# A channel mixer and a state-space convolution in one instruction order: GpSimd makes the weights' low parts from slot 14 on, two table loads are booked, and the order is drawn up again

## The chip, the cores and the metric

The kernel runs on one core of one Trainium2 chip. The metric is the device time of one launch in microseconds (us). Before the change three runs gave 1084.74, 1084.84 and 1085.39 us, with a median of 1084.84 us.

Five engines work at once, each through its own queue in program order: PE (TensorE: matmuls, with its weight loads shown as PEld), DVE (VectorE), ACT (ScalarE), POOL (GpSimd) and SP (which only issues DMAs here). POOL and ACT issue DMAs too. An instruction waits on semaphores for what other engines must have done, and everything behind it in its own queue waits with it.

## The reference

The reference normalises the 2048 rows of `u` (576 channels each) and sends them down two branches. One is a state-space convolution over the sequence (an S4D layer, by FFT), the other a two-layer mixer with 4608 hidden units:

```python
def reference(A_u, A_log_A_real, A_A_imag, A_C_real, A_C_imag, A_log_dt, A_D_skip, B_x, B_w1, B_b1, B_w2, B_b2):
    def _A_ref(u, log_A_real, A_imag, C_real, C_imag, log_dt, D_skip):
        L = u.shape[1]
        dt = jnp.exp(log_dt)
        A = -jnp.exp(log_A_real) + 1j * A_imag
        C = (C_real + 1j * C_imag) * dt[:, None]
        pos = (lambda x, dt: x.astype(dt))(jnp.arange(L), log_dt.dtype)
        P = jnp.exp((A * dt[:, None])[:, :, None] * pos[None, None, :])
        K = 2.0 * jnp.einsum("dn,dnl->dl", C, P).real
        ...
        y = jnp.fft.irfft(Uf * Kf[None, :, :], L2)[:, :, :L]
        ...
        return y + u * D_skip[None, None, :]

    def _B_ref(x, w1, b1, w2, b2):
        y = _layernorm(x, axis=-1)
        h = _gelu(jnp.einsum("bsd,df->bsf", y, w1) + b1)
        return jnp.einsum("bsf,fd->bsd", h, w2) + b2

    x = A_u
    xn = _layernorm(x, axis=-1)
    s = _A_ref(xn, A_log_A_real, A_A_imag, A_C_real, A_C_imag, A_log_dt, A_D_skip)
    g = _silu(_B_ref(xn, B_w1, B_b1, B_w2, B_b2))
    return x + s * g
```

All of it is in float32. `L` is 2048, `D` 576, `N` 128.

## The kernel before

**The mixer.** Float32 accuracy is reached with products of two parts each: a value is rounded to a high part (type fp32r) and the rest becomes a low part, and three products (high by high, high by low, low by high) are added. The mixer goes through its rows in two halves, and in each half through the 4608 hidden units in 12 groups `g` of 384, each group for two row blocks `tb` of 512. That makes 48 *slots* (`NSLOT`). A slot has 11 *positions*: three units of layer 1 (`layer1`, L508, 14 matmuls of 512 columns each, 42 in a slot) and eight of layer 2 (`layer2`, L565, 72 matmuls of 288 columns in a slot). Between them ACT applies the gelu (L541) and makes the high part `hh` (L544), and DVE makes the low part `hl` (L547). DVE adds each finished layer-2 sum to `acc` (L573). The sums lie in two PSUM tiles, `mxa` and `mxb`, which change turns, so an add has to be done before PE writes that tile again.

**The weights.** They change every second slot. A DMA on SP's queue brings a piece into `raw` (`load_raw`, L448 to L453); ACT rounds it to the high part (`split_raw`, L488) and an engine given as `low_on` subtracts to get the low part (L485). Each pair of slots has eight such pieces: five of w1 (`w1l`, 128x384; the fifth, `w1s`, has 64 partitions) and three of w2 (`w2l`, 128x576). The tiles are single, so w1's pieces are made while layer 2 of the odd slot runs, and w2's while layer 1 of the next slot runs. `split_raw(low_on=nc.vector)` defaults to DVE; only three pieces at the start are given to GpSimd. Once a low part is done, `low()` issues the next loads into the ring that it has read (`NEXT`), and these wait on SP's queue for it.

**The convolution.** It is filled in between. Its tables come from 36 blocks (`tables`: some eleven DVE and four ACT instructions each, L785 to L827), from which PE makes a piece of the kernel (`kgen`, L867, 64 small matmuls, called K below). Six chunks of 96 channels then pass forward transforms (`forward`, L939), products (`s2`, L977, with DVE L993 to L1006), inverse steps (L1030) and a last one (`i1`, L1057), whose result goes to DRAM by POOL's queue (L1068).

**The order.** One fixed order of instructions for all engines is written out by a planner, `Order`, while the kernel is traced. It holds a clock per engine (`od.t`), *lines* of steps with an engine, an estimated duration, a due time (`by`) and marks that steps need, and `od.tbl`, the activation table that ACT has by its book: a step with another `tbl` is booked with 1.28 us more. `weigh_in` books the eight weight pieces with due times counted back from the position that needs them. `od.advance` gives engines such steps as are ready and don't run into the next due time. The real hardware then runs this order with semaphores; where its times differ from the planner's, an engine waits.

**PE's visits to the convolution.** `pe_turns` runs after certain positions (`all_lines=pos in (0, 1, G + 1, G + 4, NPOS - 1)`, with `G` = 3 and `NPOS` = 11). It takes a step of the convolution when it is ready by the planner's clock. Forward and product steps (line `c1`) are held to a pace (`END`, and a share of the mean gap). A K can *ride* ahead of such a step in the same visit (`ride`, `lead`); it goes alone only when it has been ready for `ALONE` us:

```python
                if x is kl and pace["started"] and kl["steps"][0]["mark"][1] < NB - 1 and od.t["PE"] < h[1] + ALONE:
                    break
```

**Tables on ACT.** In the parameters' steps an arctangent (L709) is followed by an absolute value (L710) and a sine (L711); both functions are booked as one table, "sin". In slots 22 and 23 the finished mixer rows pass the gate's tanh (`tanh_half`, L578, booked as table "gelu"), and DVE's L589 follows.

Of the kernel before, what the change touches and what calls it, by code (L numbers as in the profile page):

```python
# [12 lines left out]
AF = mybir.ActivationFunctionType  # L13
# [22 lines left out]
G = 3  # L36
# [6 lines left out]
def dve(n):  # L43
    return 0.075 + 0.00104 * n


def act(n):
    return 0.06 + 0.00098 * n
# [159 lines left out]
def step(eng, dur, fn, need=(), mark=None, cv=0, at=0.0, late=0.0, tbl=None, by=1e9):  # L208
    return dict(eng=eng, dur=dur, fn=fn, need=tuple(need), mark=mark, cv=cv, at=at, late=late, tbl=tbl, by=by)
# [3 lines left out]
def mixer_kernel(ctx, tc, u, log_a_real, a_imag, c_real, c_imag, log_dt, d_skip, w1, b1, w2, b2,  # L213
# [249 lines left out]
    def split_raw(low_on=nc.vector):  # L463
        k = state["split"]
        state["split"] += 1
        half, g, which, i = PARTS[k]
        r = RAW.pop(k)
        if which == 1:
            if i == 0 and k:
                w1_tiles()  # L470
            h, lo, r1, r2 = W[1]
            if i < KB:
                h, lo = h[:, i], lo[:, i]
                m = P
            else:
                h, lo = r1, r2[:64]
                m = 64
        else:
            if i == 0:
                W[2] = (sb.tile([P, G, D], F32R, name="w2h"), sb.tile([P, G, D], F32R, name="w2l"))  # L480
            h, lo = W[2]
            h, lo, m = h[:, i], lo[:, i], P

        def low():
            low_on.tensor_sub(lo, r[:m], h[:m].bitcast(F32))  # L485
            for _ in range(NEXT[which - 1][i]):
                load_raw()
        nc.scalar.activation(h, r, AF.Copy)  # L488
        return low
# [85 lines left out]

    def tanh_half(z):
        t = sb.tile([P, TB], F32, name="h32", bufs=2)[:, :288]
        nc.scalar.activation(t, z, AF.Tanh, scale=0.5)  # L578
        return t

# [83 lines left out]
    def params():  # L664
# [41 lines left out]
            add("DVE", 1.9, lambda h=h: V.reciprocal(t[:, h], t[:, h]))  # L706
        add("DVE", d, lambda: V.scalar_tensor_tensor(ci, T[4], 1.0, ci, op0=OP.subtract, op1=OP.mult))
        add("DVE", d, lambda: V.tensor_mul(t, t, ci))
        add("ACT", e, lambda: A.activation(t, t, AF.Arctan), tbl="sin", late=0.0)  # L709
        add("ACT", e, lambda: A.activation(T[3], t, AF.Abs))  # L710
        add("ACT", e, lambda: A.activation(T[3], T[3], AF.Sin, bias=halfpi[:, 0:1], scale=-2.0), tbl="sin", late=0.0)  # L711
        turns(1, th)
# [456 lines left out]
    L1 = 14 * 0.2262  # L1169
    LEN = [L1] * G + [3 * n * 0.1327 for n in (4, 2, 2, 4, 3, 3, 3, 3)]  # L1170

    T0 = 12.5
    for e, t in dict(PE=0.0, ACT=4.6, DVE=3.7, POOL=3.8, SP=0.0).items():
        od.t[e] = T0 + t
    for x in od.lines:
# [86 lines left out]
        od.force(lambda: ("y2", tb, KB) in od.marks)  # L1262
        od.marks["x", tb] = od.marks["y2", tb, KB]

    def weigh_in(which):

        m = KB + 1 if which == 1 else G
        end = od.t["PE"] + sum(LEN[G:] if which == 1 else LEN[:G])
        for i in range(m):
            by = end - 0.8 * (m - i)  # L1270
            cell = []
            n = G * P if which == 1 else D
            k = len(WM)
            WM.append(which)
            wl["steps"].append(step("ACT", act(n), lambda c=cell: c.append(split_raw()), need=[("raw", k)],
                                    mark=("wh", k), by=by - 0.9, at=od.t["PE"] + od.LAT))

            def low(c=cell, k=k, n=n):
                k0 = state["load"]
                c[0]()  # L1280
                for j in range(k0, state["load"]):
                    od.marks["raw", j] = od.t["DVE"] + dve(n) + 5.5 + 1.0 * (j - k0)
            wl2["steps"].append(step("DVE", dve(n), low, need=[("wh", k)], mark=("w", k), by=by))

    WM = [1] * (KB + 1)
    for k in range(len(WM)):
# [64 lines left out]


    pace = dict(left=NCH * (2 + 2 + 4), last=0.0, started=False)
    END = 1020.0
    ALONE = 3.0

    def pe_turns(limit=1, any_time=False, all_lines=True):
        for x in (nl, pl, ml) + ((c3, c1, kl) if all_lines else ()):
            n = 0
            while n < (2 if x in (c1, nl) else limit):  # L1360
                h = od.head(x)
                if h is None or h[0]["eng"] != "PE" or h[1] > od.t["PE"] + (0.3 if x is nl else -0.2):
                    break
                if x is c1:
                    now = od.t["PE"]
                    gap = (END - now) / max(pace["left"], 1)
                    if n == 0 and pace["started"] and now < pace["last"] + 0.4 * gap and not any_time:
                        break
                    pace["started"], pace["last"] = True, now
                    pace["left"] -= 1  # L1370
                if x is kl and pace["started"] and kl["steps"][0]["mark"][1] < NB - 1 and od.t["PE"] < h[1] + ALONE:
                    break
                behind = ride(h[0]) if x is c1 or x is c3 and h[0]["mark"][0] == "i1" else None
                od.run(x)
                if behind:
                    behind()
                od.pin()
                od.advance(od.t["PE"])
                n += 1
# [52 lines left out]
    for slot in range(NSLOT):  # L1432
        turn[0] = slot + 1
        g, tb = slot // 2 % NG, slot % 2
        n = slot // 2
        final = slot >= NSLOT - 2
        for pos in range(NPOS):
            if pos < G:
                need = wmark(n, 1) + [("x", tb)]
                if pos == 0:  # L1440
                    if slot in (mid, mid + 1):
                        x_ready(tb)
                    od.force(lambda: all(m in od.marks for m in need))

                    if slot in (1, 2 * NG + 1):
                        od.marks["x", tb] -= 2.3
                cell = []
                od.unit(lambda: cell.extend([layer1(g, tb, pos)] if slot else first_layer1(pos)),
                        L1 if slot else L1 * (22, 6, 14)[pos] / 14, need)
                look_ahead(pos)  # L1450
                for k, (a, b, c) in enumerate(cell, pos + 1 - len(cell)):
                    by = hidden_by(pos, k)
                    od.urgent.append((od.t["PE"], [step("ACT", 0.62, a, tbl="gelu", by=by[0]),
                                                   step("ACT", act(TB), b, by=by[1]),
                                                   step("DVE", dve(TB), c, mark=("h", slot, k), by=by[2])]))
                od.advance(od.t["PE"])
                if pos == G - 1 and tb == 1 and slot + 1 < NSLOT:
                    weigh_in(1)
            else:
                j, terms, last, hid = l2_terms(pos - G)  # L1460
                need = [wmark(n, 2)[i] for i in hid] + [("h", slot, i) for i in hid]
                if pos == G:

                    pe_turns()
                od.force(lambda: all(m in od.marks for m in need))
                if max(od.marks[m] for m in need) > od.t["PE"] + 0.3:
                    pe_turns(any_time=True)
                cell = []
                halves = slot == NSLOT - 1 and j == 3
                od.unit(lambda: cell.append(layer2(g, tb, j, terms, last, halves)), LEN[pos], need)  # L1470
                look_ahead(pos)
                if last or halves:
                    add = cell[0]
                    dh, k = (terms[0][1], 1) if halves else (0, 2)
                    done = ("acc", slot, j, dh)
                    chain = [step("DVE", dve(288 * k), lambda: add(dh, k), mark=done, by=add_by(pos, j))]
                    if final:
                        b = 8 + 4 * tb + j
                        x = el if slot < NSLOT - 1 else od.line()
                        st = finish(b, dh * 288, (dh + k) * 288, slot == NSLOT - 1, slot == NSLOT - 1 and j > 1)  # L1480
                        st[0]["need"] = (done, ("s8", b - 8))
                        x["steps"] += st
                    elif g == NG - 1:
                        for d in range(2):
                            one, two = gate_store(4 * tb + j, d)
                            by = od.t["PE"] + 5.0
                            chain += [step("ACT", act(288), one, tbl="gelu", by=by), step("DVE", dve(288), two, by=by)]
                    od.urgent.append((od.t["PE"], chain))
                if pos == NPOS - 1 and tb == 1 and slot + 1 < NSLOT:
                    weigh_in(2)  # L1490
            for f in LATER.get((slot, pos), ()):
                f()
            od.advance(od.t["PE"])
            pe_turns(all_lines=pos in (0, 1, G + 1, G + 4, NPOS - 1))
    od.force(lambda: not od.urgent and not any(x["steps"] for x in od.lines))


# [52 lines left out]
```

## Time and profile before

| what | us |
|---|---|
| median of three runs | 1084.84 |
| the profiled execution, whole | 1084.85 |
| its span, first to last instruction | 1083.1 |
| outside of the span | 1.75 |
| PE busy | 1072.6 |
| DVE busy | 947.7 |
| ACT busy | 653.0 |
| POOL busy | 199.4 |

The profiled execution's time is the median to within 0.01 us, so sums made against it hold for the runs. Its clock was granted in full (0.998). A matmul's shown duration overlaps with the next one's, since they are pipelined. How fast PE works is therefore read from the distance of two starts, and "busy" doesn't tell a late matmul from one in time. In a view by lines, a row gives the line, engine, operation, what is written and read, shape and count, then busy time and the mean of one, then the idle time before and what ended it.

### The profile page before, as it was taken

What the parts mean: (1) busy time and instruction counts of PE and PEld (TensorE: products, weight loads), DVE (VectorE), ACT (ScalarE), POOL (GpSimd) and SP (SyncE); (2) the same over time, 40 slices, a digit from 0 to 9 for tenths busy, and PEclk for the clock granted to TensorE, in tenths of its full rate; (3) what the DMA queues carried; (4) which work ended last, traced back from release to release, by engine and by line L of the source; (5) the groups of instructions that cost most, each with busy time, mean ns of one, the idle gap of its engine ahead of it and who ended that gap; (6) DMA issues with size and microseconds to landing.
All of it is one profiled execution on the core that took longest, in us unless ns stands there. A gap on an engine that the chain in (4) does not pass through costs nothing.

```text
span 1083.1 us, 27198 instructions
## 1 busy us (share of the span) xinstructions
PE 1072.6 (99%) x11491; PEld 933.4 (86%) x11491; DVE 947.7 (88%) x1518; ACT 653.0 (60%) x974; POOL 199.4 (18%) x281
## 2 busy tenths in 40 slices
PE   9999999999999999999999999999999999999997
PEld 7989999889888888888888888888888887888896
DVE  7797878989999999999999999999999996677367
ACT  6558569767666665767756667566665754233333
POOL 6559342110000200002000010000100022110231
PEclk9999999999999999999999999999999999999999
DMA  7746455823225222454423432142312347332344
GB/s 235 231 138 191 152 196 192 215 85 116 71 70 108 67 80 58 108 94 128 134 68 99 83 85 83 37 124 47 107 53 76 111 88 238 111 105 88 96 153 117
DMA packets 136537, 125.54 MB, mean 116 GB/s; under 512 B 88156, under 2 KB 108096, under 8 KB 135392
## 3 DMA queue, kind: packets, MB, share of 16 engines
q1 hardware_dynamic: 120624, 76.44, 26.4%
q0 software_dynamic: 15040, 46.40, 13.7%
q8 instruction: 90, 1.47, 0.6%
q10 hardware_dynamic: 752, 0.97, 0.3%
q14 instruction: 31, 0.25, 0.1%
HBM read 95.52 MB, written 34.01 MB: 120 GB/s over the span
## 4 chain that ended last, share of the span: by engine, by line
PE 87%; DVE 3%; ACT 1%; issue 1%; DMA 1%; POOL 0%; ACTq 0%; DVEq 0%; POOLq 0%
PE mxa L565 19%; PE mxb L565 19%; PE mxa L508 19%; PE mxb L508 19%; PE cv L977 3%; PE cv L867 3%; PE cv L1030 2%; PE cv L939 2%; PE cv L1057 1%; DMA xn_s<-w 0%; DVE hl L547 0%; ACT L541 0%; DVE acc L573 0%; DVE A L644 0%; ACT A L741 0%
## 5 line engine op out<-in xcount | busy, mean ns | idle before, releaser
L565 PE MATMUL mxa<-w2h,hh 128*128 128x288 f32 x573 | 171.4, 299 | 0.0
L565 PE MATMUL mxb<-w2h,hh 128*128 128x288 f32 x576 | 170.9, 297 | 0.0
L565 PE MATMUL mxb<-w2h,hl 128*128 128x288 f32 x576 | 170.1, 295 | 0.2 <-DVE hl L547 0.2
L565 PE MATMUL mxb<-w2l,hh 128*128 128x288 f32 x576 | 169.5, 294 | 0.0
L565 PE MATMUL mxa<-w2h,hl 128*128 128x288 f32 x573 | 169.1, 295 | 0.0
L565 PE MATMUL mxa<-w2l,hh 128*128 128x288 f32 x573 | 168.7, 294 | 0.0
L547 DVE TENSOR_TENSOR hl<-h,hh 128x512 fp32r<-128x512 f32 x144 | 99.4, 692 | 76.3 <-ACT hh L544 75.7
L541 ACT ACTIVATE h<-mxa,b1t 128x512 f32<-128x512 f32 x73 | 50.2, 689 | 126.5 <-PE mxa L508 121.8
L767 POOL DMA_DIRECT2D par<-par_s x36 | 27.3, 759 | 518.9 <-DVE mg L810 479.1
L565 PEld LDWEIGHTS mxa<-w2h,hh 128*128 128x128 f32 x573 | 107.6, 188 | 9.6 <-issue 6.0
L565 PEld LDWEIGHTS mxb<-w2h,hh 128*128 128x128 f32 x576 | 108.2, 188 | 4.9 <-issue 2.5
L565 PEld LDWEIGHTS mxb<-w2l,hh 128*128 128x128 f32 x576 | 108.1, 188 | 0.6
L565 PEld LDWEIGHTS mxb<-w2h,hl 128*128 128x128 f32 x576 | 108.1, 188 | 0.4 <-DVE hl L547 0.4
L565 PEld LDWEIGHTS mxa<-w2l,hh 128*128 128x128 f32 x573 | 107.6, 188 | 0.7
L565 PEld LDWEIGHTS mxa<-w2h,hl 128*128 128x128 f32 x573 | 107.5, 188 | 0.0
L541 ACT ACTIVATE h<-mxb,b1t 128x512 f32<-128x512 f32 x71 | 48.9, 689 | 75.9 <-PE mxb L508 73.7
L544 ACT ACTIVATE hh<-h 128x512 fp32r<-128x512 f32 x144 | 90.9, 632 | 4.0
L573 DVE TENSOR_TENSOR acc<-mxa,acc 128x576 f32<-128x576 f32 x88 | 65.4, 743 | 17.0 <-PE mxa L565 16.7
L508 PE MATMUL mxa<-XH,w1h 128*128 128x512 f32 x284 | 80.3, 404 | 0.0
L508 PE MATMUL mxb<-XH,w1h 128*128 128x512 f32 x280 | 77.3, 398 | 0.2 <-ACT h L541 0.2
L508 PE MATMUL mxa<-XL,w1h 128*128 128x512 f32 x284 | 76.2, 390 | 0.0
L508 PE MATMUL mxa<-XH,w1l 128*128 128x512 f32 x284 | 76.0, 389 | 0.0
(230 smaller groups left out, 2422.3 us busy)
## 6 DMA issues: line engine op xcount, KB each, us to landing
raw<-in_B_w_dram SPq DMA_DIRECT2D x72, 288.0 KB, 3.5
raw<-in_B_w_dram SPq DMA_DIRECT2D x96, 192.0 KB, 3.0
par_s<-A POOLq DMA_DIRECT2D x8, 1080.0 KB, 5.9
par<-par_s POOLq DMA_DIRECT2D x36, 240.0 KB, 3.4
f2t<-f2q SPq DMA_DIRECT2D x24, 256.0 KB, 3.7
raw<-in_B_w_dram SPq DMA_DIRECT2D x48, 96.0 KB, 3.5
u_s<-in_A_u_dram POOLq DMA_DIRECT2D x16, 288.0 KB, 4.4
xc<-xn_s SPq DMA_DIRECT2D x48, 96.0 KB, 3.9
```

The costliest lines, as they stand in the source:

```text
L508: nc.tensor.matmul(q, a, b, start=j == 0, stop=j == len(ops) - 1)
L541: nc.scalar.activation(t, q, AF.Gelu_apprx_tanh, bias=b1t[:, g * G + i:g * G + i + 1], scale=1.0)
L544: LAST[0] = nc.scalar.activation(hh[:, i], t, AF.Copy)
L547: nc.vector.tensor_sub(hl[:, i], t, hh[:, i].bitcast(F32))
L565: nc.tensor.matmul(q[:, dh, :288], a[:, i, c], b[:, i, d], start=i == 0 and k == 0, stop=i == G - 1 and k == 2)
L573: nc.vector.tensor_add(o, q[:, dh:dh + n, :288], b if g == 0 else o)
L767: nc.gpsimd.dma_start(PAR[b].rearrange("p (g i) k -> p g (i k)", g=4), dram(par_s, (b // 6 * CH + b % 6 * 4) * NPAR, [[D * NPAR, P], [24 * ...
L867: nc.tensor.matmul(q[32 * g:32 * g + 32, i // 2, i % 2 * 64:i % 2 * 64 + 64], U[:, ri, 4 * g + i, :], v[:, ri, 4 * g + i, :], start=ri == ...
L939: nc.tensor.matmul(Q1ST[i, x][g // 2][64 * f:64 * f + 64, g % 2].rearrange(order), f1t[r].rearrange("p s k -> p (s k)"), rhs(r, f), start= ...
L977: nc.tensor.matmul(Q[i][32 * q:32 * q + 32, f, 2 * ri:2 * ri + 2], m[r, 4 * i + q, 32 * ri:32 * ri + 32], A2[r, 4 * p + 2 * i + q // 2, :, ...
L1030: nc.tensor.matmul(QI[q // 2][64 * f:64 * f + 64, q % 2, i], MAT["g2t", p + i // 2][r, i % 2, ri], YS[p + i // 2][0][r, i % 2, ri, f], sta ...
L1057: nc.tensor.matmul(Q[f][32 * e:32 * e + 32, t], g1t[r], A2[r, k:k + 2, 1].rearrange("p i d r -> p i r d"), start=True, stop=True, skip_gro ...
```

## The change

It has three parts. From slot 14 on, `weigh_in` gives the low parts of the weights to GpSimd, booked with 0.2 + 0.0023 n us. The arctangent is booked under a table of its own, and where the table booked isn't "gelu", the gate's tanh is preceded by a gelu of one column, which makes the gelu table the one loaded. The planner's constants are new: its start `T0`, the pace (`END`, the share 0.30), `ALONE`, how long before PE's clock a step must be ready (0.60 instead of 0.2), and the positions after which all lines are asked.

```diff
     def tanh_half(z):
         t = sb.tile([P, TB], F32, name="h32", bufs=2)[:, :288]
+        if od.tbl != "gelu":
+            nc.scalar.activation(small[:, 5:6], epst[:, 0:1], AF.Gelu_apprx_tanh)
         nc.scalar.activation(t, z, AF.Tanh, scale=0.5)
         return t
...
-        add("ACT", e, lambda: A.activation(t, t, AF.Arctan), tbl="sin", late=0.0)
+        add("ACT", e, lambda: A.activation(t, t, AF.Arctan), tbl="arctan", late=0.0)
...
-    T0 = 12.5
+    T0 = 13.2
...
-    def weigh_in(which):
-
+    SHIFT = 14
+
+    def weigh_in(which, slot=0):
+
+        e = "POOL" if slot >= SHIFT else "DVE"
         m = KB + 1 if which == 1 else G
         end = od.t["PE"] + sum(LEN[G:] if which == 1 else LEN[:G])
         for i in range(m):
-            by = end - 0.8 * (m - i)
             cell = []
             n = G * P if which == 1 else D
+            d = dve(n) if e == "DVE" else 0.2 + 0.0023 * n
+            by = end - max(0.8, d) * (m - i)
             k = len(WM)
             WM.append(which)
-            wl["steps"].append(step("ACT", act(n), lambda c=cell: c.append(split_raw()), need=[("raw", k)],
+            wl["steps"].append(step("ACT", act(n), lambda c=cell: c.append(split_raw(nc.gpsimd if e == "POOL" else nc.vector)), need=[("raw", k)],
                                     mark=("wh", k), by=by - 0.9, at=od.t["PE"] + od.LAT))
 
-            def low(c=cell, k=k, n=n):
+            def low(c=cell, k=k, d=d):
                 k0 = state["load"]
                 c[0]()
                 for j in range(k0, state["load"]):
-                    od.marks["raw", j] = od.t["DVE"] + dve(n) + 5.5 + 1.0 * (j - k0)
-            wl2["steps"].append(step("DVE", dve(n), low, need=[("wh", k)], mark=("w", k), by=by))
+                    od.marks["raw", j] = od.t[e] + d + 5.5 + 1.0 * (j - k0)
+            wl2["steps"].append(step(e, d, low, need=[("wh", k)], mark=("w", k), by=by))
...
-    END = 1020.0
-    ALONE = 3.0
+    END = 1010.0
+    ALONE = 7.0
...
-                if h is None or h[0]["eng"] != "PE" or h[1] > od.t["PE"] + (0.3 if x is nl else -0.2):
+                if h is None or h[0]["eng"] != "PE" or h[1] > od.t["PE"] + (0.3 if x is nl else -0.60):
                     break
...
-                    if n == 0 and pace["started"] and now < pace["last"] + 0.4 * gap and not any_time:
+                    if n == 0 and pace["started"] and now < pace["last"] + 0.30 * gap and not any_time:
...
-                    weigh_in(1)
+                    weigh_in(1, slot)
...
-                    weigh_in(2)
+                    weigh_in(2, slot)
...
-            pe_turns(all_lines=pos in (0, 1, G + 1, G + 4, NPOS - 1))
+            pe_turns(all_lines=pos in (0, 1, 2, G + 1, G + 3, NPOS - 1))
```

## The prediction

> **What bounds the kernel now.** I read the page first, then PE by lines and by its chain, then the places where PE changes between mixer and convolution, and last what DVE and POOL do beside it.
>
> ```profile
> PE 1072.6 (99%) x11491; PEld 933.4 (86%) x11491; DVE 947.7 (88%) x1518; ACT 653.0 (60%) x974; POOL 199.4 (18%) x281
> ...
> 194.50:907.50 713.00, 712.41 (x8868) 613.36 (x8867) 681.52 (x1058) 461.17 (x680) 66.90 (x108) 1.00 0.35 92
> ...
> 13.10:1076.00 1062.90, 474.76 (x3456) 462.82 (x3456) 1.00 0.41 114
> ...
> 13.10:1076.00 1062.90, 467.90 (x1974) 365.08 (x1974) 1.00 0.41 114
> ...
> 1054.56 2.38 PE mxb L565 x18
> ...
> 1063.30 3.17 PE mxa L508 x14
> ```
>
> The second row is a stretch from the first K to the last; its columns after the length are the busy time of PE, PEld, DVE, ACT and POOL. The next two are L565 alone and L508 alone. PE is the bound, and it is bound by work that the change leaves alone: 3456 matmuls of layer 2 at 2.38 / 18 = 0.132 us make 457 us, and layer 1's 2016 (the 1974 and slot 0's 42) at 3.17 / 14 = 0.226 make 456 us, together 913 of the 1063 us in which PE runs the stream. DVE is the second engine, 96% busy (681.52 / 713) while tables are made. POOL has 91% of that stretch free. What can be gained lies in the other 150 us, of which most is the convolution's own matmuls. The rest is what PE loses at a change, and true waits.
>
> ```profile
> 665.20 0.29 PE L565 MATMUL mxb<-w2h,hl 128*128 128x288 f32 x1
> 665.43 1.10 PE L867 MATMUL cv<-v,U 128*32 128x64 f32 x64
> 666.46 0.40 PE L565 MATMUL mxb<-w2h,hh 128*128 128x288 f32 x1
> 666.70 0.30 PE L565 MATMUL mxb<-w2l,hh 128*128 128x288 f32 x1
> 666.83 0.29 PE L565 MATMUL mxb<-w2h,hl 128*128 128x288 f32 x1
> ...
> 559.59 1.10 PE L867 MATMUL cv<-v,U 128*32 128x64 f32 x64
> 560.62 1.62 PE L977 MATMUL cv<-A,f2t 64*32 64x192 f32 x64
> 562.17 1.21 PE L508 MATMUL mxa<-XH,w1h 128*128 128x512 f32 x4
> ```
>
> Two mixer matmuls start 0.13 us apart (666.70 to 666.83). Around a K that goes alone the steps are 0.23 (665.20 to 665.43) and 0.24 (666.46 to 666.70), so each visit costs 0.10 + 0.11 = 0.21 us beside its work. A K that rides, as at 559.59, takes the same 1.03 us and pays for no visit of its own. True waits are rare: I find two of over 0.2 us in the mixer's stream, shown below.
>
> **The change part by part, against the profiled 1084.85 us** (0.01 from the median).
>
> *Rides.* All 36 K's run in any order; what changes is how many open a visit of their own.
>
> ```profile
> 194.57 1.10 PE L867 MATMUL cv<-v,U 128*32 128x64 f32 x64
> ...
> 330.01 1.10 PE L867 MATMUL cv<-v,U 128*32 128x64 f32 x64
> ...
> 334.43 1.59 PE L977 MATMUL cv<-A,f2t 64*32 64x192 f32 x64
> ...
> 889.71 1.10 PE L867 MATMUL cv<-v,U 128*32 128x64 f32 x64
> ...
> 894.13 1.62 PE L1057 MATMUL cv<-A,g1t 64*32 64x384 f32 x32
> ...
> 906.44 1.10 PE L867 MATMUL cv<-v,U 128*32 128x64 f32 x64
> ```
>
> Along PE's timeline 21 of the 36 K's go alone, the first at 194.57, the last at 906.44. Three run before the first forward step, where `ALONE` doesn't apply; 18 are left. Of these, nine are followed by a step that could have carried them within 4.1 to 4.8 us: the first at 330.01 (host 4.4 us on), the last at 889.71 (host 4.4 us on). Each had been ready for 3 us by the planner's clock. With `ALONE` at 7 it may wait 4 us more, and the visits come at coarse places, so these nine are in reach. The new positions 2 and G + 3 give one visit more per slot, which I take as two riders more: 11 x 0.21 = -2.3 us. Bounds: nothing, and all 18, -3.8 us. Five of the present 15 rides could be lost as hosts move, +1.0.
>
> *Booked table loads.* The loads themselves run today; the booking moves steps around them.
>
> ```profile
> 96.97 1.28 ACT L541 ACT_TABLE_LOAD   x1
> 98.26 0.69 ACT L541 ACTIVATE h<-mxb,b1t 128x512 f32<-128x512 f32 x1
> ...
> 98.39 0.39 PE L508 MATMUL mxa<-XR,w1s 128*128 128x512 f32 x1
> 99.00 1.21 PE L508 MATMUL mxb<-XH,w1h 128*128 128x512 f32 x4 [0.23 <-ACT h L541]
> ...
> 509.46 1.28 ACT L578 ACT_TABLE_LOAD   x1
> ...
> 523.04 0.40 PE L565 MATMUL mxb<-w2h,hl 128*128 128x288 f32 x1 [0.19 <-DVE hl L547]
> ```
>
> After the arctangent ACT runs late, the gelu starts at 98.26, and PE steps 0.61 us instead of 0.23 (98.39 to 99.00): 0.38 lost. At 523.04, after a gate's tanh that loaded a table of its own (509.46), PE waits for `hl`: 0.48 to the matmul before it instead of 0.13, 0.35 lost. A restart costs some 0.1 more each time. With ACT's clock right, the planner has no reason to put these steps so close: I take both, -0.9 us. Bounds: 0, if something else comes late in their place, and -0.9, since no other such wait exists. The one-column gelus lie on ACT, 60% busy, and each saves a load of 1.28 us there; nothing for PE, and if ACT had no time to spare each would still be paid by the load that it saves.
>
> *Low parts on GpSimd.* The odd slots from 15 to 45 call `weigh_in` 16 times for each layer: 80 pieces of w1 and 48 of w2.
>
> ```profile
> L485 DVE TENSOR_TENSOR w2l<-raw,w2h 128x576 fp32r<-128x576 f32 x72 | 50.5, 748 | 1.9 <-ACT w2h L488 1.7
> ...
> L485 DVE TENSOR_TENSOR w1l<-raw,w1h 128x384 fp32r<-128x384 f32 x94 | 47.6, 556 | 0.0
> ...
> L485 POOL TENSOR_TENSOR w1l<-raw,w1h 128x384 fp32r<-128x384 f32 x2 | 2.0, 1023 | 0.0
> ...
> L1068 POOL DMA_DIRECT2D s_s<-pr x24 | 14.0, 590 | 97.1 <-ACT pr L1065 97.1
> ...
> 335.80 1.75 ACT L488 ACTIVATE w1h<-raw 128x384 fp32r<-128x384 f32 x4
> ...
> 342.92 1.22 DVE L823 TENSOR_TENSOR v<-w,mg 128x1024 f32<-128x1024 f32 x1
> 344.06 0.75 DVE L573 TENSOR_TENSOR acc<-mxb,acc 128x576 f32<-128x576 f32 x1
> ...
> 345.59 1.09 PE L508 MATMUL mxb<-XH,w1h 128*128 128x512 f32 x4
> ```
>
> DVE is spared 80 x 0.556 + 48 x 0.748 = 80 us. POOL takes 80 x 1.02; for the 576 columns no row stands, and in proportion it is 1.53, together 155 us. Are the weights still in time? In slot 15 the high parts run from 335.80; five low parts in a row from the first, at 336.3, end at 341.4. PE begins the next slot at 345.59 and reads `w1l` eight matmuls (1.8 us) later, 6.0 us of room. For w2, 3 x 1.53 = 4.6 us fit a layer 1 of 9.5. What is queued on POOL ahead of them: a chunk's result in two times four stores at 0.59, 4.7 us, still within 6.0; a parameter load; at the end the outputs. Behind a low part SP's next weight loads wait, as they wait for DVE today, and they have a slot's time. So the direct cost is 0; bounds 0 and, with all of it late by a store group, see the rivals.
>
> The indirect cost is that the two engines may hold each other up.
>
> ```profile
> 40.10 2.29 POOL L395 TENSOR_SCALAR A<-A,U 128x576 f32<-128x576 f32 x1
> ...
> 40.37 1.10 DVE L547 TENSOR_TENSOR hl<-h,hh 128x512 fp32r<-128x512 f32 x1 [3.65 <-ACT hh L544]
> ...
> 42.84 0.69 DVE L547 TENSOR_TENSOR hl<-h,hh 128x512 fp32r<-128x512 f32 x1 [0.39 <-ACT hh L544]
> ```
>
> Behind a POOL operation begun 0.27 us before, `hl` took 1.10 us instead of 0.69: held for 0.41. In slot 15's window the add at 344.06 ends at 344.81, and PE writes that tile at 345.59: 0.78 to spare. Bounds for one low part: nothing, and its whole 1.02 us. I take 0.41, which is measured, for two DVE operations in each of the 16 windows of w1: 0.82 - 0.78 = 0.04, x 16 = +0.6 us. DVE's 80 us as such are worth nothing to PE, which doesn't wait for them now.
>
> [...]
>
> *The end.*
>
> ```profile
> 1076.45 0.45 DVE L573 TENSOR_TENSOR acc<-cv,acc 128x288 f32<-128x288 f32 x1
> ...
> 1077.48 0.45 DVE L644 SCALAR_TENSOR_TENSOR A<-A,row 128x288 f32<-128x288 f32 x1
> ...
> 1078.18 0.44 ACT L639 ACTIVATE row<-acc 128x288 f32<-128x288 f32 x1 [1.84 <-DVE A L644]
> ```
>
> The last half's silu waits for a buffer until 1077.93 though its sum is done at 1076.90, 1.0 us. The change doesn't touch these steps; 0, bounds -1.0 and +1.0 for another order of buffers. The new `T0`, pace and margin of 0.60 only pick other places.
>
> Sum: -2.3 - 0.9 + 0.6 = -2.6, and 1084.85 - 2.6 = **1082.2 us**; its own range is 1080.3 (all riders, no holding) to 1083.6 (half the riders, one of the two waits).
>
> **The rivals.**
>
> *GpSimd holds DVE where an add is due: slower.* The place is the 16 windows of layer 2 in odd slots. The table operations (as L823 at 342.92) read two SBUF tiles, as `hl` does, and stand just ahead of the adds. It decides from 0.78 us of holding per window. One operation held for a whole low part: 1.02 - 0.78 = 0.24, x 16 = 3.8 us; two held for 0.71, the middle of 0.41 and 1.02: 0.65 x 16 = 10.4 us. The middle, 7 us, on 1082.2 gives 1089. For it: the planner fills DVE to the due time and books nothing for it. Against: the 2.8 us of low parts that left DVE in the same window.
>
> *The weights themselves come late: slower.* Each held by a table operation, five low parts at 1.02 + 1.22 (L823's length) take 11.2 us, all of the room from 336.3 to 347.4; four stores of 0.59 ahead of them make the weights 2.4 us late. Where three chunks' stores fall into such a window: 1082.2 + 3 x 2.4 = 1089.4. Against: the holding would have to come each time.
>
> *It does little.* Ready K's find no host, since the hosts wait for K's themselves, and other waits replace the two: 1084.85 - 0.5 = 1084.3. For it: eleven K's must find places that the trace only suggests.
>
> *More than that.* All 18 ride, both waits go, the last buffer is free: -3.8 - 0.9 - 1.0, 1079.2 us.
>
> **How the numbers follow.** The forecast gets 0.52, the holding 0.17, late weights 0.05, little 0.18, more 0.08. The range of 8 in 10 reaches from 1079.5, which leaves out half of the last, to 1088.5, which leaves out the upper part of the slower two. Some 0.2%, 2.2 us, is what can be told from no change. Faster than 1082.7: most of the forecast (0.45) and "more" (0.08), 0.53. Within: a little of the forecast (0.07) and most of "little" (0.16), 0.23. Slower than 1087: the two slower cases and a rest, 0.24.
>
> **What would show it.** Rides: lone L867 groups on PE fall from 21 to about 10. Booking: no PE wait over 0.2 us at the sine and at the gate; L578 shows no load of its own. Low parts: L485 on POOL at 1.0 and 1.5 us, 128 more of them, and PE's steps into `mxa` and `mxb` stay at 0.13 and 0.23. It is wrong if PE shows new waits ended by DVE's L573 or L547, or by POOL's L485, and above all if POOL's L485 or DVE's table operations grow by half a microsecond.

## The result, and the profile after

The changed kernel takes 1128.79 us (median of five, 1127.96 to 1130.86) where the kernel before took 1084.74 beside it: a ratio of 1.0411 [1.0399, 1.0422]. It is 44 us slower; 1082.2 was forecast, and 1088.5 was the end of the range. The profiled execution took 1128.21, with a clock of 0.992.

The head of its page:

```profile
span 1126.4 us, 27224 instructions
...
PE 1085.5 (96%) x11491; PEld 940.6 (84%) x11491; DVE 961.5 (85%) x1390; ACT 643.6 (57%) x968; POOL 378.1 (34%) x409
```

DVE has lost 128 instructions, 79 us by their lengths, and yet it is busy for longer than before (961.5 against 947.7). PE is busy for 96% of the span instead of 99%: the new time is waiting, mostly.

By lines, with the shapes kept apart (busy time and mean ns of one behind the first bar, idle time before behind the second):

```profile
L547 DVE TENSOR_TENSOR hl<-h,hh 128x512 fp32r<-128x512 f32 x144 | 110.1, 768 | 81.8 <-ACT hh L544 81.1
...
L485 POOL TENSOR_TENSOR w1l<-raw,w1h 128x384 fp32r<-128x384 f32 x66 | 83.2, 1286 | 182.8 <-ACT w1h L488 155.3 <-DMA row<-y_s 27.3
L485 POOL TENSOR_TENSOR w2l<-raw,w2h 128x576 fp32r<-128x576 f32 x48 | 78.2, 1652 | 61.4 <-ACT w2h L488 61.3
L573 DVE TENSOR_TENSOR acc<-mxb,acc 128x576 f32<-128x576 f32 x88 | 65.7, 747 | 16.2 <-PE mxb L565 16.0
L825 DVE TENSOR_TENSOR v<-w,mg 128x1024 f32<-128x1024 f32 x36 | 51.6, 1433 | 0.0
L812 DVE TENSOR_TENSOR mg<-par 128x1024 f32<-128x1024 f32 x36 | 50.8, 1411 | 0.8
...
L1000 DVE TENSOR_TENSOR pr<-cv,kk 128x768 f32<-128x768 f32 x48 | 45.4, 945 | 0.0
```

The low parts on POOL are longer than forecast (1.29 and 1.65 us; 1.02 and 1.53). DVE's operations that read two tiles in SBUF have grown, `hl`, `v` and `mg` by 11 to 18% in the mean (what they take undisturbed is in the first experiment). Those that read one operand from PSUM, the add L573 (`mxb`) and L1000 (`cv`), have not: 43 such operations overlap a low part on POOL, and none of them takes over 0.01 us longer for it.

One window of w1 on the timeline (start and length in us), first DVE, then POOL, then PE; the last row is of another place, for the last section:

```profile
785.17 0.74 DVE L573 TENSOR_TENSOR acc<-mxb,acc 128x576 f32<-128x576 f32 x1
785.84 5.48 DVE L823 TENSOR_TENSOR U<-w,mg 128x1024 f32<-128x1024 f32 x1
791.24 0.74 DVE L573 TENSOR_TENSOR acc<-mxa,acc 128x576 f32<-128x576 f32 x1
...
786.33 2.95 POOL L485 TENSOR_TENSOR w1l<-raw,w1h 128x384 fp32r<-128x384 f32 x3
789.24 0.99 POOL L485 TENSOR_TENSOR w1s<-raw,w1r 64x384 fp32r<-64x384 f32 x1
...
788.36 0.29 PE L565 MATMUL mxb<-w2h,hl 128*128 128x288 f32 x1
792.04 0.61 PE L565 MATMUL mxa<-w2h,hh 128*128 128x288 f32 x1 [3.39 <-DVE acc L573]
792.45 0.45 PE L565 MATMUL mxa<-w2l,hh 128*128 128x288 f32 x1
792.68 0.45 PE L565 MATMUL mxa<-w2h,hl 128*128 128x288 f32 x1
...
795.47 0.29 PE L565 MATMUL mxa<-w2h,hl 128*128 128x288 f32 x1
795.60 0.30 PE L565 MATMUL mxa<-w2h,hh 128*128 128x288 f32 x1
...
466.61 0.40 PE L565 MATMUL mxa<-w2h,hh 128*128 128x288 f32 x1 [1.90 <-DVE acc L573]
```

The table operation L823 takes 5.48 us instead of 1.22. It ends at 791.32, 1.09 us behind POOL's last piece (789.24 + 0.99 = 790.23): it was held not for one piece but through four that followed each other. (This is one of the longest holds; most end with one piece, as counted below.) The add behind it starts only at 791.24, though its matmuls had ended before 788.4, and PE, which needs the tile `mxa` again, stands from 788.36 to 792.04. That is 3.68 us where the step is 0.13. Then comes a second loss: to 795.33 the steps are 0.24 us instead of 0.13, about 1.7 us more. The granted clock is 0.50 there (791.9 to 795.3), which is called half clock below.

Where all of it lies, by the view of waits (us in total, times, longest):

```profile
PEld mxa L565 <- DVE hl L547: 12.2, 13, 2.3
PE mxa L565 <- DVE hl L547: 9.4, 9, 2.0
PEld mxa L565 <- DVE acc L573: 8.6, 7, 3.6
PE mxa L565 <- DVE acc L573: 6.9, 6, 3.4
```

PE and PEld wait for the same things, so the two aren't added. Worked out from PE's timeline: between two matmuls of the mixer the steps that exceed the usual one by over 0.15 us sum to 36.5 us in 40 places; before it was 0.7 us in two. The smaller excesses grow by 6.1 us, mostly at half clock: there are four stretches of 3.4 us, at most 1.7 lost in each, 6.8 in all, of which 1.4 (seven steps of layer 1 behind 546) are in the 36.5 already. The visits to the convolution take 2.2 us more than before, and the first of these matmuls starts 0.5 us earlier. This makes up the 43.5 us by which the mixer's last matmul starts later (1119.2 against 1075.7).

### The profile page after: what moved, and what is told of

Read it like the earlier page. It is cut to its first block, busy times and chain, and to the rows that moved or that the text cites. A ratio compares the mean times of both kernels' runs of the same rounds, so it can differ in the third digit from the quotient of the medians.

```text
span 1126.4 us, 27224 instructions
## 1 busy us (share of the span) xinstructions
PE 1085.5 (96%) x11491; PEld 940.6 (84%) x11491; DVE 961.5 (85%) x1390; ACT 643.6 (57%) x968; POOL 378.1 (34%) x409
## 4 chain that ended last, share of the span: by engine, by line
PE 69%; DVE 25%; issue 2%; ACT 2%; DMA 1%; POOL 0%; DVEq 0%; ACTq 0%; POOLq 0%
PE mxa L508 16%; PE mxb L565 15%; PE mxa L565 15%; PE mxb L508 14%; DVE acc L573 3%; PE cv L869 2%; DVE mg L812 2%; DVE hl L547 2%; PE cv L979 2%; DVE w L787 2%; PE cv L941 1%; DVE pr L1000 1%; DVE v L825 1%; PE cv L1032 1%; DVE v L829 1%
## 5 line engine op out<-in xcount | busy, mean ns | idle before, releaser
L565 PE MATMUL mxa<-w2h,hl 128*128 128x288 f32 x573 | 171.9, 300 | 9.4 <-DVE hl L547 9.4
L547 DVE TENSOR_TENSOR hl<-h,hh 128x512 fp32r<-128x512 f32 x144 | 110.1, 768 | 81.8 <-ACT hh L544 81.1
L485 POOL TENSOR_TENSOR w1l<-raw,w1h 128x384 fp32r<-128x384 f32 x66 | 83.2, 1286 | 182.8 <-ACT w1h L488 155.3
L541 ACT ACTIVATE h<-mxa,b1t 128x512 f32<-128x512 f32 x73 | 50.0, 686 | 116.5 <-PE mxa L508 116.0
L485 POOL TENSOR_TENSOR w2l<-raw,w2h 128x576 fp32r<-128x576 f32 x48 | 78.2, 1652 | 61.4 <-ACT w2h L488 61.3
L541 ACT ACTIVATE h<-mxb,b1t 128x512 f32<-128x512 f32 x71 | 48.8, 687 | 81.8 <-PE mxb L508 77.1
L488 ACT ACTIVATE w2h<-raw 128x576 fp32r<-128x576 f32 x72 | 45.1, 676 | 62.6 <-PE mxa L565 33.5
L573 DVE TENSOR_TENSOR acc<-mxa,acc 128x576 f32<-128x576 f32 x88 | 65.4, 743 | 17.8 <-PE mxa L565 17.4
```

The source lines that it names most:

```text
L541: nc.scalar.activation(t, q, AF.Gelu_apprx_tanh, bias=b1t[:, g * G + i:g * G + i + 1], scale=1.0)
L547: nc.vector.tensor_sub(hl[:, i], t, hh[:, i].bitcast(F32))
L565: nc.tensor.matmul(q[:, dh, :288], a[:, i, c], b[:, i, d], start=i == 0 and k == 0, stop=i == G - 1 and k == 2)
L573: nc.vector.tensor_add(o, q[:, dh:dh + n, :288], b if g == 0 else o)
```

## The experiments

Each was timed beside the kernel before (1084.8 to 1085.2 in these runs). "Holds" are counted as follows: a DVE operation with two SBUF inputs that takes over 0.1 us more than it does in the first experiment. In the changed kernel there are 80 after 295 us, 79.9 us in all, median 0.82. Of these, 74 end with a single low part; in 48 of the 74 the next low part has begun by then, but it waits for DVE in its turn. Six go on through two to five low parts, up to 4.77 us, and make 20 of the 79.9 us. But single holds add up too: from 729.85 to 736.07 four low parts hold four operations of DVE one by one, 3.1 us in sum, ahead of the add for which PE waits longest (3.6 us, to 737.60). "Mixer's end" is the start of its last matmul, which leaves out what follows it. Theory 1, in the runs on the low parts, says that a low part on GpSimd, which reads two tiles, holds a DVE operation with two SBUF inputs to its end, as 74 of these 80 holds have it, and so takes from DVE about what it spared it (79.9 us of holding, 79 us of low parts), in places where PE then waits.

**GpSimd writes but doesn't read.** The order of all engines stays that of the changed kernel; each low part on GpSimd becomes two memsets. The low parts of the weights from slot 14 on are zeros.

```diff
-            low_on.tensor_sub(lo, r[:m], h[:m].bitcast(F32))
+            if low_on is nc.gpsimd and half + g:
+                low_on.memset(lo.bitcast(F32), 0.0)
+                low_on.memset(lo.bitcast(F32), 0.0)
+            else:
+                low_on.tensor_sub(lo, r[:m], h[:m].bitcast(F32))
```

> The changed kernel, but GpSimd only writes the low parts (two memsets of zero each, which leaves the weights' low parts out of the product) and reads nothing; DVE, ACT and PE have the same instructions in the same order as in the changed kernel. [...] Rival 5 (GpSimd's being slow and late, or the planner's filling DVE too tightly, is enough for the loss without any holding): over 1110 us. [...]

1083.84 us (eight runs), ratio 0.9991 [0.9981, 1.0002]. Its page and its view by lines (its line numbers are 4 higher):

```profile
PE 1071.8 (99%) x11491; PEld 933.7 (86%) x11491; DVE 883.3 (82%) x1390; ACT 643.6 (59%) x968; POOL 316.5 (29%) x537
...
L551 DVE TENSOR_TENSOR hl<-h,hh 128x512 fp32r<-128x512 f32 x144 | 99.5, 693 | 100.5 <-ACT hh L548 99.7
...
L816 DVE TENSOR_TENSOR mg<-par 128x1024 f32<-128x1024 f32 x36 | 44.0, 1221 | 0.8
L829 DVE TENSOR_TENSOR v<-w,mg 128x1024 f32<-128x1024 f32 x36 | 43.7, 1215 | 0.0
...
L577 DVE TENSOR_TENSOR acc<-mxb,acc 128x576 f32<-128x576 f32 x88 | 65.9, 749 | 23.6 <-PE mxb L569 23.2
L1004 DVE TENSOR_TENSOR pr<-cv,kk 128x768 f32<-128x768 f32 x48 | 45.4, 946 | 0.0
...
L486 POOL MEMSET w1l<- 128x384 f32 x64 | 26.9, 420 | 155.7 <-PE mxa L512 155.7
```

No hold is left: `hl` is at 693 ns instead of 768, `mg` at 1221 instead of 1411, `v` at 1215 instead of 1433; the operations with one operand in PSUM take the same as in the changed kernel (749 and 946 ns, there 747 and 945). DVE does the same 1390 instructions in 883.3 us instead of 961.5; 78 us of its busy time were holding. The time falls by 1128.79 - 1083.84 = 45 us. POOL is as present as before, in the same order, and writes the same tiles; what is gone is its reading from SBUF (and some of its time: two memsets take 0.84 us, the subtraction 1.29; the memsets also don't wait for ACT's high part, as the last row shows). So the loss is not the order, not the low parts' place and not the planner's constants. By the view of waits PE waits 1.0 us in all for pieces of w1, at 532 to 534.

**The new `weigh_in` alone**, in the kernel before (`SHIFT = 14`, without the booked table loads and the new constants).

> The kernel before with the new weigh_in alone (GpSimd from slot 14), all constants and bookings as before. Theory 1: 1120 to 1140 us, and DVE's instructions with two SBUF inputs grow by 70 to 90 us in sum, those that read PSUM by nothing. Rival 2: within 1083 to 1090 us.

1149.77 us, ratio 1.0596 [1.0575, 1.0617], more than expected. Its waits:

```profile
PE mxb L565 <- DVE acc L573: 14.6, 6, 4.5
PE mxb L508 <- ACT h L541: 8.1, 4, 3.5
PE mxa L565 <- DVE hl L547: 6.5, 7, 2.5
```

The same waits as in the changed kernel, and more of a kind that is small there: PE waits for ACT's gelu L541 for 8.1 us into `mxb` of layer 1 (0.2 in the changed kernel). DVE has 69 holds, 71.4 us. Ten stretches at half clock lose at most some 17 us. So this part alone makes the kernel 65 us slower; with the rest of the change it is 21 us less.

**The rest alone**: all but the low parts.

```diff
-    SHIFT = 14
+    SHIFT = 48
```

> The changed kernel, but DVE makes all low parts again (SHIFT at 48): new constants, booked table loads and rides stay. [...] Rival 2 (the order drawn up with the new constants is bad in itself): still over 1110 us. Rival 3 (both a part): between 1090 and 1110.

1096.65 us, ratio 1.0107 [1.009, 1.0124]: slower than by the prediction's own terms of rides and booking (1084.8 - 2.3 - 0.9 = 1081.6), and in the range of Rival 3. The mixer's end comes at 1072.6, 3.1 us earlier than before, with no wait over 0.15 us. What is late is the convolution. Its last piece on PE and then POOL's queue:

```profile
1036.15 1.26 PE L1059 MATMUL cv<-A,g1t 64*32 64x384 f32 x24
...
1039.05 2.34 POOL L1070 DMA_DIRECT2D s_s<-pr  x4 [64.22 <-ACT pr L1067]
...
1043.67 0.76 POOL L604 DMA_DIRECT2D row<-u_s  x1
...
1060.70 0.77 POOL L604 DMA_DIRECT2D row<-u_s  x1
...
1076.73 0.73 POOL L604 DMA_DIRECT2D row<-u_s  x1
...
1084.98 2.13 POOL L616 DMA_DIRECT2D out_dram<-row  x4 [6.10 <-DVE row L613]
```

And the kernel before there:

```profile
1013.41 0.91 PE L1057 MATMUL cv<-A,g1t 64*32 64x384 f32 x16
...
1016.27 2.35 POOL L1068 DMA_DIRECT2D s_s<-pr  x4 [30.16 <-ACT pr L1065]
...
1020.90 0.76 POOL L602 DMA_DIRECT2D row<-u_s  x1
...
1039.06 0.78 POOL L602 DMA_DIRECT2D row<-u_s  x1
```

The last result is stored 22.8 us later. Behind it come rounds of loading rows, multiplying and storing, about 16 us each (1043.67, 1060.70, 1076.73), and the third now lies behind the mixer's end: 22 us from the last matmul to the end of the span instead of 7. The new constants thus hold the convolution back so long as the planner's DVE is full; in the order of the changed kernel, in which the planner's DVE is relieved, it ends in time (7 us from the last matmul to the end).

**The rest with milder constants.**

```diff
-    SHIFT = 14
+    SHIFT = 48
...
-    ALONE = 7.0
+    ALONE = 5.0
...
-                if h is None or h[0]["eng"] != "PE" or h[1] > od.t["PE"] + (0.3 if x is nl else -0.60):
+                if h is None or h[0]["eng"] != "PE" or h[1] > od.t["PE"] + (0.3 if x is nl else -0.2):
...
-                    if n == 0 and pace["started"] and now < pace["last"] + 0.30 * gap and not any_time:
+                    if n == 0 and pace["started"] and now < pace["last"] + 0.4 * gap and not any_time:
```

> The low parts all on DVE as in e1, with the changed kernel's bookings, start and positions, but a K waits at most 5 us for a ride, the pace's share is 0.40 and the readiness margin 0.2 again. e1's stream of mixer matmuls ended 3.1 us earlier than before, and only its convolution came late (last inverse step at 1036 us instead of 1013). Theory 1 (rides and booked loads are worth what the prediction said, the rest of e1's loss is the late convolution): 1080.5 to 1082.5 us, 12 or 13 K's alone, the last convolution step near 1012. Rival (the new order loses elsewhere too): 1084 us or more.

1081.95 us (seven runs), ratio 0.9972 [0.996, 0.9983]: this beats both kernels. Twelve K's go alone instead of 21, PE visits the convolution 81 times instead of 90, the mixer's end is at 1072.9 and the last visit at 1009.4, early enough. Three constants were changed together, and which of them lets the convolution end sooner was not separated; the share of 0.40 alone asks for longer distances between visits than 0.30, not for shorter ones.

**The booking alone**, in the kernel before: arctangent under its own table, gelu of one column ahead of the gate's tanh.

> The kernel before with the arctangent's own table booked and the one-column gelu ahead of the gate's tanh, nothing else. The prediction's term: -0.9 us, 1083.9 to 1084.2, and no wait of PE over 0.2 us at the sine and at the gate. Rival: other waits take their place, 1084.6 to 1085.2.

1083.6 us (eleven runs), ratio 0.9989 [0.998, 0.9997], -1.2 us (by the interval -0.3 to -2.2); -0.9 was forecast, and the time lies 0.3 below the expected range. PE and ACT near the sine, and the view of the gate's line L580:

```profile
98.32 0.39 PE L508 MATMUL mxa<-XR,w1r 128*128 128x512 f32 x1
98.55 0.39 PE L508 MATMUL mxa<-XR,w1s 128*128 128x512 f32 x1
98.77 1.07 PE L508 MATMUL mxb<-XH,w1h 128*128 128x512 f32 x4
...
95.99 1.28 ACT L541 ACT_TABLE_LOAD   x1
97.28 0.69 ACT L541 ACTIVATE h<-mxb,b1t 128x512 f32<-128x512 f32 x1
...
L580 ACT ACTIVATE h<-acc x16: 427/440/447, 502.9 to 533.3; 128x288 f32<-128x288 f32 x16
L580 ACTq EVENT_SEMAPHORE  x5: 17/17/17, 507.7 to 530.3; - x5
```

The gelu stands 1.49 us ahead of the matmul that waits for it (97.28 to 98.77) where it stood 0.74 ahead before, and the step of 0.61 is 0.22. The gate's tanh has no table load of its own. In all of PE's mixer stream a single step is left that is over 0.15 us too long (0.2 us); both waits are gone, as forecast.

**Which low parts cost?** The changed kernel with only w1's 80 pieces on GpSimd, or only w2's 48:

```diff
-        e = "POOL" if slot >= SHIFT else "DVE"
+        e = "POOL" if slot >= SHIFT and which == 1 else "DVE"
```

> The changed kernel with the 80 pieces of w1 on GpSimd, the 48 of w2 on DVE. The planner's convolution comes as late here as in e1 (its last step at 1037 us), so some 12 us belong to that. Theory 1: DVE's two-input instructions grow by 80 x 0.62 = 50 us in sum, no more than 1.0 us for each piece that stands by itself and whole strings of up to five; in time about 1112 us (1100 to 1125).

```diff
-        e = "POOL" if slot >= SHIFT else "DVE"
+        e = "POOL" if slot >= SHIFT and which == 2 else "DVE"
```

> The changed kernel with the 48 pieces of w2 on GpSimd, the 80 of w1 on DVE; the planner's convolution ends in time (1008 us). Theory 1: DVE's two-input instructions grow by some 35 us; the holds of 1.5 us fall on layer 1, where hl stands, so 1095 to 1108 us. If only w1's place under the adds matters (the prediction's rival), within 1081 to 1086.

With w1 alone 1131.62, ratio 1.043 [1.0411, 1.0449], 42 holds of 34.7 us in all, the mixer's end at 1113.5; with w2 alone 1102.6, ratio 1.0162 [1.0144, 1.0181], 37 holds of 47.4 us, the mixer's end at 1095.2. The first is 6.6 us above the expected range, the second lies within it. Against 1072.6 without either, that is 40.9 us for 80 pieces and 22.6 for 48, 0.51 and 0.47 us for each. Per piece both kinds cost about the same, though w1's 80 pieces hold DVE for less time than w2's 48. Part of this is the half clock (31 us long with w1 alone, 7 with w2 alone); the rest I put down to where the holds fall. The whole times also hold the late convolution (17 us behind the mixer's end with w1 alone), so they can't be compared as they stand; and the two costs sum to 63.5 us where both together cost 46.6, so they don't simply add. With w1 alone the two rows of interest are:

```profile
L547 DVE TENSOR_TENSOR hl<-h,hh 128x512 fp32r<-128x512 f32 x144 | 99.6, 693 | 89.4 <-ACT hh L544 88.8
...
L825 DVE TENSOR_TENSOR v<-w,mg 128x1024 f32<-128x1024 f32 x36 | 53.5, 1486 | 0.0
```

`hl` isn't held at all (693, as undisturbed), the table operations are; the adds come late behind these. It is the prediction's first rival, with its place. That place isn't all of it, since w2's pieces, which are made during layer 1, cost 22.6 us alone.

**Does it take strings of pieces?** Every other piece on GpSimd (80 of 128), with the pace's share and the margin of the milder constants, so that single pieces stand apart.

```diff
-        e = "POOL" if slot >= SHIFT else "DVE"
...
         for i in range(m):
+            e = "POOL" if slot >= SHIFT and i % 2 == 0 else "DVE"
```

> The changed kernel with every other piece on GpSimd (the first, third and fifth of w1, the first and third of w2: 80 of 128), the rest on DVE; pace share 0.40 and margin 0.2, so that the planner's convolution comes in time (1024 us). No two GpSimd pieces of a layer follow each other directly. Theory 1a (each piece holds DVE once, whether pieces stand in strings or not): two-input instructions grow by some 50 us, the time is 1100 to 1112 us. Theory 1b (the loss comes from the strings, through which DVE stays held for 3 to 5 us): no instruction is held for over 1.9 us, no stretch at half clock, and under 1095 us.

1122.03 us, ratio 1.034 [1.0319, 1.0361], 10 us above the range of Theory 1a. There are 56 holds, 43.9 us, the longest 2.4, and three stretches at half clock. The theory that the strings make the loss falls: one piece at a time is enough. The mixer's end is at 1105.4, 32.8 us after 1072.6; another 15 us follow it, since the convolution ended late (last visit 1053.8) in a plan that books a relief which DVE doesn't get.

**Fewer pieces.** `SHIFT = 30` in the changed kernel (64 pieces), and `SHIFT = 40` in the version with milder constants (24 pieces, where DVE is no longer full: without them it is busy for 65% of the time from 900 to 1070 us, against 96% from 300 to 910).

> The changed kernel with SHIFT at 30: 8 of the 16 pairs of slots have their low parts on GpSimd. Theory 1: the loss over e1 halves, some 1081.6 + 47 / 2 = 1105 us (1098 to 1112). Rival 2: no change from 1128.8. Rival 4 (one bad place, such as the mid of the kernel around 541 us or the end at 1085 us, makes most of the loss): if the mid, under 1095 us; if the end, over 1115 us.

> e6 (the faster one) with the low parts on GpSimd from slot 40 on, when the tables are done and DVE is half idle: 3 of the 16 pairs of slots, 24 pieces. Theory 1: a piece costs where a two-input instruction stands in its way; with DVE half idle that is about half as often, 24 x 0.63 / 2 = 8 us of holding and some 1 to 4 us of time, 1083 to 1086 us. If holding only matters where DVE is full: 1081.5 to 1082.5, the time of e6.

From 30: 1100.41, ratio 1.0141 [1.0121, 1.0161], 33 holds; the mixer's end at 1090.9, so 18.3 us for 64 pieces, 0.29 each. From 40: 1082.5 (ten runs), ratio 0.9979 [0.9969, 0.9988], five holds of 7.5 us in all and one wait of PE of 1.05 us; the mixer's end is at 1073.1 (1072.9 without the pieces), no loss against 0.9972 that these runs can tell. So a piece has no fixed price: in the changed kernel 79.9 us of holding cost 46.6 us, here 7.5 us cost 0.3. As I read it, the price is what DVE has queued behind the hold, and a DVE with room takes the hold out of its idle time.

## Why the prediction was wrong

**Rides: right.** 21 lone K's have become 9, "about 10" was forecast, and visits fell from 90 to 78. In the rest alone there are eight visits fewer (82), 8 x 0.21 = 1.7 us by the prediction's price. The mixer's end moved by 3.1 there, and by 1.6 in the booking alone (1074.1); the difference is 1.5. No run has the rides alone, so their price is shown by this difference only.

**Booking: right**, -1.2 where -0.9 was forecast. Together with the rides it is the 2.9 us of the version with milder constants.

**Low parts: mis-sized, and this decides.** The step was "I take 0.41, which is measured, for two DVE operations in each of the 16 windows of w1: 0.82 - 0.78 = 0.04, x 16 = +0.6 us." The runs show 45 us. Three things in it were off:

- *The size of one hold.* 0.41 came from `hl` behind a GpSimd TENSOR_SCALAR, which reads one tensor. The low part reads two, and behind it DVE waited for the whole instruction. Count back from the end of a held operation by the time that it takes undisturbed, and you are 0.12 to 0.15 us ahead of the end of a low part on POOL (5% to 95% of the 80), as if the operation had been let go there. The row at 40.10 also misled me: there `hl` was through at 41.47 (40.37 + 1.10), before the POOL operation's end at 42.39 (40.10 + 2.29), and that says nothing of another operation with other operands. Why the TENSOR_SCALAR let `hl` go early was not tried.
- *The upper bound.* "Nothing, and its whole 1.02 us" took one hold to end with one piece. That holds for 74 of the 80 (a piece of w2 takes more than 1.02 us, though), but six stay held through pieces that follow each other, up to 4.77 us, as at 785.84, and single holds add up where they follow each other, as the 3.1 us ahead of PE's longest wait do. A bound from one operation was no bound for a string.
- *The count.* Two in each window of w1, none for w2. The runs have 80 holds, and w2's pieces alone cost 22.6 us.

The mechanism was on the list: the first rival names the place (adds behind held table operations in layer 2 of odd slots) and the 0.78 us from which it decides. At 1089 and a chance of 0.17 it had the right sign, but a price of 7 us where 45 came. Its ground against, "the 2.8 us of low parts that left DVE in the same window", was the other error. By the instructions' lengths DVE was spared 79 us, and 80 us came back as holding; by its busy time, in which overlapping starts count once, it was spared 66 (949.4 in the rest alone, 883.3 where GpSimd only writes) and got 78 back. An engine full before the change was full after it, now in places that the planner doesn't know of.

The runs give 80 holds where GpSimd reads, 74 of them to the end of a single low part, and none where it only writes. The prediction had gone by one row with other operands.

**Half clock: missing from the prediction.** In four places, after waits, PE ran at half clock (0.50 granted) for 3.4 us each, at most 6.8 us of the 44 in all.

**The constants.** "The new `T0`, pace and margin of 0.60 only pick other places" was wrong as well, hidden in the changed kernel: with DVE still full they make the end 15 us longer.

**Late weights: right to be small.** PE's waits that end with POOL's L485 sum to 1.5 us in the changed kernel, in four places from 543 to 546, to 2.5 us with w1 alone (the longest 1.2) and to 1.8, in one place, with w2 alone; where GpSimd only writes, the longest is 0.3.

**The range.** Two figures of its own range don't follow from its terms: all riders and both waits give 1084.85 - 3.8 - 0.9 = 1080.15, not 1080.3, and half the riders with one wait give 1083.2, or 1083.9 with the 0.6 of holding, not 1083.6. Neither changes the forecast.

## What to carry to other kernels

Work moved from VectorE to GpSimd may not relieve VectorE at all: here, where operations of both read two tiles from SBUF, the time came back as holding (79 us spared, 79.9 held), at moments that the plan didn't know. VectorE's operations with one operand in PSUM weren't held (at most 0.01 us in 43), nor was any beside a GpSimd that only writes (`hl` at 693 ns instead of 768), and where VectorE had idle time the holding cost next to nothing (0.3 us for 7.5); other pairs of operations were not tried. A bound for such contention has to come from an operation with the same operands, and has to allow for several in a row (five at most here). A twin of the kernel in which GpSimd only writes, in the same order, tells in one run what the contention costs; and when several edits come together, each alone (here the booking and the rides, 2.9 us) may be worth keeping.

## What the hardware showed

*GpSimd is held too.* Its low part of w1 takes 1.29 us in the mean, against 0.98 in the undisturbed string above (2.95 us for three). In the changed kernel 72 of its 128 low parts take over 0.1 us longer than undisturbed, 35 us in all. Counted back in the same way, 71 of them were let go 0.10 to 0.15 us ahead of the end of a DVE operation with two SBUF inputs. So the two engines mostly take turns: a piece holds an operation of DVE, and that operation holds the next piece.

*Half clock after a wait.* Stretches of 20 us in the changed kernel; behind the busy times of PE, PEld, DVE, ACT and POOL stand the granted clock, the share of the DMA engines and GB/s:

```profile
460.00:480.00 20.00, 18.04 (x155) 15.96 (x155) 16.17 (x28) 9.89 (x17) 0.00 (x0) 0.91 0.32 62
...
780.00:800.00 20.00, 16.61 (x150) 15.22 (x155) 19.90 (x23) 11.29 (x18) 9.07 (x8) 0.91 0.27 67
```

In the first, POOL does nothing. PE had waited there for an add (466.61, 1.90 us): the last row of the timeline shown above. DVE's view there has the add behind the table operation L823, which waited 1.68 us for ACT's L806 and its table load. The twin that only writes has the same order and no such wait: as I read it, engines that were held elsewhere no longer have the plan's times when they come here. From 467.7 on the steps are 0.24 us for 3.4 us, at a granted clock of 0.50. Before it lie this wait of 1.9 us and two late steps (0.36 and 0.24 us instead of 0.13) some 4 us earlier. The other three stretches begin at 546.2, 737.3 and 791.9: behind four waits of 0.2 to 0.5 us within 3 us, and in waits of 3.6 and 3.4 us; the clock granted in the 3.4 us from there is 0.50 each time. Waits of 2.2 us (to 648.87) and 2.0 us (to 916.63) had no such stretch behind them (1.00 granted in the 3.4 us after each), so the length of a wait alone doesn't decide. What exactly sets it off was not tried.
